# A first MLP whose last two token blocks share one in-projection through seven block products

## The chip, the cores and the metric

The kernel runs on one core of a Trainium2 chip. The metric is the device time of one execution in microseconds, as the median of several runs. A core has TensorE (PE: the matmul engine), VectorE (DVE), ScalarE (ACT), GpSimd (POOL) and SyncE (SP), which here issues the DMA transfers between DRAM and the on-chip memory in the order of its queue.

## What is computed

Retention attention gives 1536 tokens of 512 values; a first MLP with a gate (512 to 2048 to 512) and, behind an RMS norm, a second gated MLP (512 to 1536 to 512) follow.

```python
B, H, S, D = 2, 8, 768, 64
for t in range(S):                                  # attention
    state = gamma * state + outer(k[:, :, t], v[:, :, t])
    y[:, :, t] = scale * q[:, :, t] @ state
x = y as [1536, 512]
h = x @ w_in                                        # first MLP
x = (h * sigmoid(1.702 * h)) @ w_out
xn = x / sqrt(mean(x * x) + 1e-6) * rms_g           # second MLP
g = xn @ w_gate
out = (g * sigmoid(g) * (xn @ w_val)) @ w_out2
```

The weights arrive as 64-bit floats. Products are made in split form: each float32 operand is a high and a low part, and a product is three matmuls (high by high, high by low, low by high).

## The kernel before

**Tiles.** The tokens are three blocks of 512 (0, 1, 2), each of four chunks of 128 tokens for the attention. An MLP1 step (block j, f) takes one of 16 slices of 128 of the 2048 inner values: `mlp1_in` (line 400) makes h with the 12 matmuls of `in_proj` (L392), `mlp1_act` (406) the gate and its two halves on ACT and DVE (L408, L410, L411), and `mlp1_out` (415) adds the slice's part to the block's four sums with 12 matmuls (L369 to L371). All of these are 128x512.

**Weights.** SP loads half tiles of 64-bit words (`load_next`, L140), and `convert_next` (144) turns one of them into float32 with two ACT operations (L168, L169) and three DVE operations (L172, L173, L179). `halves` (373) splits a value: an ACT copy (L374) and a DVE subtraction (L375). In each step `split_in` and `split_out` (200, 204) split the in-weights of two steps on and the out-weights of the step, each 128x512; with 48 steps a slice is split once for every block. The 68 half tiles are converted beside MLP1 and the first part of MLP2, at a pace counted per step; those of MLP2 are written to DRAM and loaded again (`reload`, 187).

**Order.** `STEPS` (line 38) lists 48 steps: block 0 with f 0 to 7, block 1 with all, block 0 with f 8 to 15, block 2 with all. The attention of chunks 0 to 3 stands ahead; that of chunks 4 to 7 lies beside the first eight steps, that of 8 to 11 beside the second half of block 0, one task of `attention` (832) in a step, a chunk in two. A chunk has two POOL products (L230, L237) and a DVE operation for the low half of x (`x_low`, 319). The norms (`norm_tasks`, 446) and the operand sums of MLP2 (`x_tasks`, 502) lie beside block 2. A scheduler places each instruction in its engine's line from the order in which the code writes it and from the buffers of its pools: four 64-bit half tiles (`st`), two split out-weights (`wo`), four split in-weights (`wa`), fourteen temporary tiles (`tmp`).

**Seven products.** MLP2 already takes two blocks together through `seven` (655): a 2x2 arrangement of blocks of weights by blocks of tokens is made with seven products instead of eight, from sums of weight blocks (`set_tasks`, 571) and sums of token blocks (`x_tasks`). A product is 6 matmuls of 128x512 (L666) that add up in two banks; the results come out as sums with ACT copies (L673) and DVE additions. Two such chains run in turns, one in the banks of `ps_h`, one in those of `ps_t`; between them `fill` items do out-products.

## Time and profile before

| | us |
|---|---|
| median of 3 runs (602.67 to 603.08) | 602.86 |
| the profiled execution | 603.59 |
| its span on the core | 601.8 |
| PE busy | 594.8 |
| DVE busy | 445.5 |
| ACT busy | 356.2 |

The span is the time from the first to the last event of the core in the profiled execution; that execution's own time also has what lies around the span. Busy time is what an engine spends in instructions, an operation from its start to its end. Where instructions of an engine overlap, a single one's duration is longer than its share of the line; the distance from one start to the next (here: the pitch) is then the cost. The granted clock (PEclk) is TensorE's: 1.00 is 2.4 GHz.

### The profile page before, as it was taken

To read this page: it belongs to the slowest core of one execution; us is meant where nothing else is said; L and a number is where in the kernel's file an instruction comes from. 1 tells how busy PE (TensorE), PEld (TensorE's weight loads), DVE (VectorE), ACT (ScalarE), POOL (GpSimd) and SP (SyncE) were. 2 spreads that over 40 slices of the span, in tenths; PEclk is the share of its full clock that TensorE was granted. 3 is DMA by queue.
4 is the path that set the end of the run, shared out by engine and by line. 5 is a ranking of instruction groups with operands and counts; after the bars stand their busy time and mean duration, and the time that the engine had idled before them with its cause. 6 is when DMAs were issued, how large, how long until landed. Compare 5 with 4: busy or idle time off the path is not lost.

```text
span 601.8 us, 9259 instructions
## 1 busy us (share of the span) xinstructions
PE 594.8 (99%) x3354; PEld 495.2 (82%) x3354; DVE 445.5 (74%) x805; ACT 356.2 (59%) x685; POOL 29.6 (5%) x28
## 2 busy tenths in 40 slices
PE   8999999999999999999999999999999999999997
PEld 6777888888888878888887888898989889988885
DVE  2999968897797868989977999774655766655542
ACT  2577777786675666867757675453534535544532
POOL 4404100000112000000000000000000000000000
PEclk9999999999999999999999999999999999999999
DMA  8966724564577535436523513240211376643521
GB/s 328 354 207 245 247 87 139 162 203 133 179 228 244 175 118 149 114 106 205 180 106 105 174 54 116 78 139 20 95 63 71 108 256 230 211 143 106 173 71 70
DMA packets 32877, 93.14 MB, mean 155 GB/s; under 512 B 3904, under 2 KB 4160, under 8 KB 32832
## 3 DMA queue, kind: packets, MB, share of 16 engines
q1 hardware_dynamic: 32400, 92.42, 46.7%
q8 instruction: 26, 0.43, 0.3%
q10 hardware_dynamic: 432, 0.14, 0.1%
q14 instruction: 19, 0.16, 0.1%
HBM read 73.67 MB, written 18.87 MB: 154 GB/s over the span
## 4 chain that ended last, share of the span: by engine, by line
PE 94%; DVE 3%; DMA 1%; ACT 1%; issue 0%; SPq 0%; DVEq 0%
PE h L392 21%; PE acc L369 8%; PE acc L370 7%; PE acc L371 7%; PE o L369 5%; PE o L370 5%; PE o L371 5%; PE y L299 2%; PE sc L257 2%; PE y L286 1%; PE g2a L666 1%; PE g0a L666 1%; PE v0a L666 1%; PE v2a L666 1%; PE g10a L666 1%; PE g8a L666 1%
## 5 line engine op out<-in xcount | busy, mean ns | idle before, releaser
L369 PE MATMUL acc<-gh,woh 128*128 128x512 f32 x192 | 76.5, 399 | 0.0
L370 PE MATMUL acc<-gl,woh 128*128 128x512 f32 x192 | 74.9, 390 | 0.3 <-DVE gl L411 0.3
L371 PE MATMUL acc<-gh,wol 128*128 128x512 f32 x192 | 74.9, 390 | 0.0
L374 ACT ACTIVATE wih<-w 128x512 fp32r<-128x512 f32 x48 | 30.2, 631 | 56.5 <-PE h L392 53.2
L370 PE MATMUL o<-w3l,gh 128*128 128x512 f32 x144 | 56.2, 391 | 0.0
L369 PE MATMUL o<-w3h,gh 128*128 128x512 f32 x144 | 56.2, 391 | 0.0
L371 PE MATMUL o<-w3h,gl 128*128 128x512 f32 x144 | 56.1, 389 | 0.0
L375 DVE TENSOR_TENSOR wil<-w,wih 128x512 fp32r<-128x512 f32 x48 | 34.5, 719 | 20.6 <-ACT wih L374 20.4
L173 DVE CUSTOM_DVE_ANT_0 qw<-qw,uw 128x1024 uint16<-128x1024 uint16 x68 | 48.2, 712 | 0.6
L168 ACT ACTIVATE qw<-w 128x512 f32<-128x512 f32 x68 | 45.1, 663 | 0.6 <-DMA w<-in_w 0.6
L169 ACT ACTIVATE uw<-w 128x512 uint32<-128x512 uint32 x68 | 45.2, 665 | 0.0
L369 PEld LDWEIGHTS acc<-gh,woh 128*128 128x128 f32 x192 | 36.0, 188 | 8.6 <-issue 0.2
L370 PEld LDWEIGHTS acc<-gl,woh 128*128 128x128 f32 x192 | 36.1, 188 | 7.7 <-DVE gl L411 0.7
L374 ACT ACTIVATE woh<-w 128x512 fp32r<-128x512 f32 x48 | 30.1, 628 | 20.6 <-DVE w L179 13.8
L371 PEld LDWEIGHTS acc<-gh,wol 128*128 128x128 f32 x192 | 36.0, 188 | 7.6
L375 DVE TENSOR_TENSOR wol<-w,woh 128x512 fp32r<-128x512 f32 x48 | 32.8, 684 | 6.0 <-ACT woh L374 5.9
L375 DVE TENSOR_TENSOR gl<-gw,gh 128x512 fp32r<-128x512 f32 x24 | 16.6, 692 | 27.3 <-ACT gh L374 27.2
L172 DVE TENSOR_SCALAR qw<-qw 128x512 uint32<-128x512 uint32 x68 | 29.9, 441 | 8.8 <-ACT qw L168 8.8
L411 DVE SCALAR_TENSOR_TENSOR gl<-g,gh 128x512 fp32r<-128x512 f32 x48 | 34.1, 709 | 2.5 <-ACT gh L410 0.8
L374 ACT ACTIVATE gh<-gw 128x512 fp32r<-128x512 f32 x24 | 15.1, 631 | 29.0 <-PE o L370 24.9
L371 PEld LDWEIGHTS o<-w3h,gl 128*128 128x128 f32 x144 | 27.0, 188 | 5.6
L369 PEld LDWEIGHTS o<-w3h,gh 128*128 128x128 f32 x144 | 27.1, 188 | 4.8 <-ACT w3h L374 0.2
(1111 smaller groups left out, 1507.7 us busy)
## 6 DMA issues: line engine op xcount, KB each, us to landing
w<-in_w SPq DMA_DIRECT2D x68, 512.0 KB, 4.6
qk<-in_qk SPq DMA_DIRECT2D x12, 512.0 KB, 6.5
kv<-in_kv SPq DMA_DIRECT2D x12, 512.0 KB, 7.1
g0d<-gs SPq DMA_DIRECT2D x12, 256.0 KB, 2.0
g2d<-gl SPq DMA_DIRECT2D x12, 256.0 KB, 2.1
gw<-g0d SPq DMA_DIRECT2D x12, 256.0 KB, 2.7
gw<-g2d SPq DMA_DIRECT2D x12, 256.0 KB, 2.7
out<-o SPq DMA_DIRECT2D x11, 256.0 KB, 2.4
```

What stands on the lines that cost most here:

```text
L168: nc.scalar.activation(out=q, in_=high.bitcast(F32), func=ACTF.Copy, scale=2.0 ** -112)
L169: nc.scalar.activation(out=t, in_=low, func=ACTF.Copy, scale=2.0 ** -29)
L172: lambda: nc.vector.tensor_scalar(out=m, in0=m, scalar1=3, scalar2=None, op0=ALU.logical_shift_left),
L173: lambda: nc.vector.tensor_tensor(out=m, in0=m, in1=t, op=ALU.add),
L369: nc.tensor.matmul(out=out, lhsT=ah, rhs=bh, start=first, stop=False)
L370: nc.tensor.matmul(out=out, lhsT=ah, rhs=bl, start=False, stop=False)
L371: nc.tensor.matmul(out=out, lhsT=al, rhs=bh, start=False, stop=last)
L374: nc.scalar.activation(out=hi, in_=src, func=ACTF.Copy)
L375: nc.vector.tensor_tensor(out=lo, in0=src, in1=hi.bitcast(F32), op=ALU.subtract)
L392: nc.tensor.matmul(out=ps, lhsT=w[a][:, k * 128:(k + 1) * 128], rhs=x[b][:, k, :], start=o == order[0], stop=o == order[-1])
L411: nc.vector.scalar_tensor_tensor(out=lo, in0=g, scalar=1.0 / GELU, in1=hi.bitcast(F32), op0=ALU.mult, op1=ALU.subtract)
L666: nc.tensor.matmul(out=bank, lhsT=u, rhs=v, start=first and k == 0 and x == 0, stop=k == 1 and x == 2, skip_group_check=True,)
```

## The change

MLP1 is laid out anew. Block 0 runs through all 16 slices in a row (`for f in range(F1)`), with two conversions in a step and the attention of all eight remaining chunks beside it, one task in a step and a second one at f = 4 and f = 9. Its out-weights are split once, in a tile of 128x1024, and written to DRAM (512 KB a slice); the converted in-weights are written too (256 KB a slice). x of blocks 1 and 2 stays unsplit (`xr1`, `xr2`).

Then blocks 1 and 2 go through the in-projection as a pair: eight passes p of two slices, each a chain `seven` of seven products, in two lanes that stand three products apart (`LAG`). The token operands (four sums, seven splits of 128x1024, `m_tasks`) are made at the end of block 0 and through the first pass, the weight operands pass by pass (`set_tasks("wm", p)`). The gate of block 1 is split and its out-products run as `fill` items between the chains, with the split out-weights loaded again (`load_wo`, names `wowp`). The gate of block 2 is written to DRAM (`gm`, 256 KB a slice) and its out-products run in a last stretch of 16 steps of 12 matmuls, with gate (`gwm`) and weights (`wowq`) loaded again. The norm of block 0 lies beside the pair, that of block 1 and `x_tasks` beside the last stretch. Ten conversions more than before lie in MLP2. The diff, cut to its core:

```diff
...
-HALF = F1 // 2
-PARTS = [(0, 0, HALF), (1, 0, F1), (0, HALF, F1), (2, 0, F1)]
-STEPS = [(j, f, f == a, f == b - 1) for j, a, b in PARTS for f in range(a, b)]
-
-
-FIRST, OTHER, LAST = 1, 0, 2
+FIRST, OTHER, LAST = 0, 1, 2
+LAG = 3
...
-    wo_p = pool("wo", 2)
+    wo_p = pool("wo", 3)
...
-    tmp_p = pool("tmp", 14)
+    tmp_p = pool("tmp", 12)
...
+        elif half == 0:
+            p = i // 2
+            if i % 2 == 0:
+                kept["wm", p] = tc.dram_tile([128, 1024], F32, name=f"wm{p}d")
+            c = (i % 2) * 512
+            nc.sync.dma_start(out=kept["wm", p][:, c:c + 512], in_=dst.bitcast(F32))
...
+    def split_out(f):
+        t = wo_p.tile([128, 1024], F32R, tag="wo", name=f"wo{f}")
+        parts["wo", f] = both(t)
+        halves(*both(t), raw["w1", f][:, 512:1024].bitcast(F32))
+        kept["wo", f] = tc.dram_tile([128, 1024], F32, name=f"wo{f}d")
+        nc.sync.dma_start(out=kept["wo", f], in_=t.bitcast(F32))
+    def load_wo(f, user):
+        t = wo_p.tile([128, 1024], F32R, tag="wo", name=f"wo{user}{f}")
+        parts[user, f] = both(t)
+        nc.sync.dma_start(out=t.bitcast(F32), in_=kept["wo", f])
...
+            elif j == 1:
+                xt[j] = [x1_p.tile([128, KD, T], F32, tag="x11", name="xr1")]
+            else:
+                xt[j] = [xt_p.tile([128, KD, T], F32, tag="xt1h", name="xr2")]
...
-        x_low(c)
+        at.pop(("y", c))
...
+    def mlp1_item(key, j, f, m):
+        if j not in acc:
+            acc[j] = [psum(ps_a, f"acc{j}_{i}") for i in range(KD)]
+        w, g = parts[key, f], gt[key, f]
+        product(acc[j][m], [t[:, m * 128:(m + 1) * 128] for t in w], g, f == 0, f == F1 - 1)
...
+    def m_tasks():
+        xop["m"] = ops = {}
+        own = {1: "xt1l", 3: "xt0h", 4: "xt0l"}
+        def b(h, j):
+            return xt[1 + j][0][:, 2 * h:2 * h + 2, :]
+        def split(i, src):
+            if i in own:
+                t = xt_p.tile([128, KD, T], F32R, tag=own[i], name=f"xm{i}")
+                h, l = t[:, 0:2, :], t[:, 2:4, :]
+            else:
+                h, l = wide(f"xmh{i}", F32R), wide(f"xml{i}", F32R)
+            halves(h, l, src)
+            ops[i] = (h, l)
+        return sums_and_splits(b, split, lambda n: wide(f"m{n}"), lambda n: wide(f"m{n}"), b(0, 1))
...
+        if kind == "wm":
+            row = lambda i: raw["wm", g][:, 512 * i:512 * i + 512]
...
+    def use_m(p):
+        def use(i, j, src, own):
+            f = 2 * p + i
+            if j == 0:
+                nc.scalar.activation(out=own, in_=src, func=ACTF.Silu, scale=GELU)
+                gate_parts(("wp", f), own)
+                load_wo(f, "wp")
+                fill.extend((f, m) for m in range(KD))
+            else:
+                t = later["gs"].tile([128, T], F32, tag="gs", name=f"gm{f}")
+                nc.scalar.activation(out=t, in_=src, func=ACTF.Silu, scale=GELU)
+                to_dram("m", f, t)
+        return use
...
-    for i, (j, f, first, last) in enumerate(STEPS):
-        if i == 0:
-            att = [x for c in range(CPB, 2 * CPB) for x in attention(c)]
-        if i == HALF + F1:
-            att = [x for c in range(2 * CPB, 3 * CPB) for x in attention(c)]
+    att = [x for c in range(CPB, B * NC) for x in attention(c)]
+    sets = {}
+    def start_set(p):
+        reload("wm", p)
+        sets[p] = deque(set_tasks("wm", p))
+    def some(tasks, n):
+        for _ in range(min(n, len(tasks))):
+            tasks.popleft()()
+    for f in range(F1):
         begun = len(nc.cur_bb.bb.instructions)
-        k = min(i, len(STEPS) - 5)
-        if k <= HALF:
-            pace = min(2 * k + 4, k + HALF + 1, 2 * HALF)
-        elif k < F1:
-            pace = 2 * HALF + 13 * (k - HALF) // 8
-        else:
-            pace = k + HALF + 3 + (min(k, 32) - 8) // 3
-        while i and count["converted"] < pace:
+        while f and count["converted"] < min(2 * f + 4, 2 * F1):
             convert_next()
-        split_out(i)
-        if i:
-            split_in(i + 2)
-        ps = mlp1_in(i)
+        split_out(f)
+        if f:
+            split_in(f + 2)
+        if f == F1 - 3:
+            start_set(0)
+        if f == F1 - 2:
+            phase.close()
+            later["wb"] = side(ctx, "wb", 3)
+            later["gs"] = side(ctx, "gs", 3)
+            mops = deque(m_tasks())
+            start_set(1)
+            some(mops, 1)
+            some(sets[0], 1)
+        if f == F1 - 1:
+            some(mops, 4)
+            some(sets[0], 3)
...
+        if f in (4, 9):
+            next_of(att)
+    assert not att
+    lanes = [[(p, n) for p in range(k, F1 // 2, 2) for n in range(7)] for k in range(2)]
+    chains = {
+        p: seven(f"m{p}", ("wm", p), use_m(p), (ps_h, ps_t)[p % 2], xop["m"], T) for p in range(F1 // 2)
+    }
+    order = []
+    for t in range(len(lanes[0]) + LAG):
+        for k in range(2):
+            if 0 <= t - k * LAG < len(lanes[0]):
+                order.append(lanes[k][t - k * LAG])
...
+    mlp1_out("wo", 0, F1 - 1)
+    for m in range(KD):
+        evacuate(0, m)
+    norm = deque(norm_tasks(0, ps_h))
+    need = (1, 2, 5, 7, 8, 9, 11)
+    for e, (p, n) in enumerate(order):
+        if p == 0:
+            some(mops, need[n] - (11 - len(mops)))
+            if n < 3:
+                some(sets[0], 5)
+            some(sets[1], 2)
+        chains[p][n]()
+        while len(fill) > 4:
+            f, m = fill.popleft()
+            mlp1_item("wp", 1, f, m)
+        if p + 2 < F1 // 2:
+            if n == 0:
+                start_set(p + 2)
+            if n in (2, 3, 4, 5, 6):
+                some(sets[p + 2], 1)
+        if e > 12 and e % 2:
+            if count["converted"] < 2 * F1 + 20:
+                convert_next()
+        if e in (24, 32):
+            some(norm, 1)
+    some(norm, 1)
+    def wait_m(f):
+        if f < F1:
+            t = waiting["m", f] = later["gs"].tile([128, T], F32, tag="gs", name=f"gwm{f}")
+            nc.sync.dma_start(out=t, in_=kept_g["m", f])
+            load_wo(f, "wq")
+    def gate_m(f):
+        if f < F1:
+            gate_parts(("wq", f), waiting.pop(("m", f)))
+    while fill:
+        f, m = fill.popleft()
+        mlp1_item("wp", 1, f, m)
+        if f == F1 - 1:
+            evacuate(1, m)
+    some(norm, 1)
+    wait_m(0)
+    wait_m(1)
+    gate_m(0)
+    tasks = None
+    for f in range(F1):
+        wait_m(f + 2)
+        gate_m(f + 1)
+        some(norm, 2 if f == 0 else 1)
+        if f == 0:
+            norm += norm_tasks(1, ps_t) + x_tasks()
+        if f in (4, 6, 8, 10, 12):
+            some(norm, 1)
+        if f == 8:
+            for x in range(2):
+                reload("w2", x)
+        if f == 10:
+            sets = [set_tasks(k, 0) for k in ("wg", "wv")]
+        if f in (11, 13):
+            t = sets[(f - 11) // 2]
+            t[1]()
+            t[2]()
+        if f == F1 - 1:
+            some(norm, len(norm))
+            for n in (0, 3, 4):
+                for t in sets:
+                    t[n]()
+        mlp1_out("wq", 2, f)
...
-        for n in (1, 7, 13) if g >= JOIN else (1, 7):
+        for n in (1, 4, 7, 10) if g >= JOIN else (1, 4, 7):
...
```

How instructions stand on their engines, at three places. First PE in MLP1 after its first third: before, a step of block 2 (`h2_5` is its h of slice 5, `acc2_0` its first sum; `xt2h` and `xt2l` are the halves of x, `wih`/`wil` and `woh`/`wol` the split weights). Rows of before:

```order
L392 MATMUL h2_5_2868<-xt2l_1996,wih37_2728 128x512
L392 MATMUL h2_5_2868<-xt2h_1995,wil37_2729 128x512
L392 MATMUL h2_5_2868<-xt2h_1995,wih37_2728 128x512
L392 MATMUL h2_5_2868<-xt2l_1996,wih37_2728 128x512
L392 MATMUL h2_5_2868<-xt2h_1995,wil37_2729 128x512
L369 MATMUL acc2_0_2626<-gh36_2808,woh36_2785 128x512
L370 MATMUL acc2_0_2626<-gl36_2809,woh36_2785 128x512
L371 MATMUL acc2_0_2626<-gh36_2808,wol36_2786 128x512
```

Rows of after: the pair (`m3b` is the second bank of pass 3, `xmh2` and `xml2` the split token operand 2, `wm3xh` a split weight operand, `acc1_0` the first sum of block 1).

```order
L712 MATMUL m3b_2156<-xmh2_1687,wm3xh_1919 128x512
L712 MATMUL m3b_2156<-xml2_1688,wm3xh_1919 128x512
L712 MATMUL m3b_2156<-xmh2_1687,wm3xl_1920 128x512
L712 MATMUL m3b_2156<-xmh2_1687,wm3xh_1919 128x512
L712 MATMUL m3b_2156<-xml2_1688,wm3xh_1919 128x512
L712 MATMUL m3b_2156<-xmh2_1687,wm3xl_1920 128x512
L382 MATMUL acc1_0_1878<-gh3_2076,wowp3_2080 128x512
L383 MATMUL acc1_0_1878<-gl3_2077,wowp3_2080 128x512
L384 MATMUL acc1_0_1878<-gh3_2076,wowp3_2080 128x512
L382 MATMUL acc1_1_1879<-gh3_2076,wowp3_2080 128x512
```

A product of six matmuls on one operand stands where twelve on the four quarters of x stood, and block 1's out-products follow between two products of the chains.

Second, DVE where the second of the three block stretches begins. Before (`wol27`, `wil31`: low halves of out- and in-weights; `gl27`: of the gate; `qw`: conversion):

```order
L173 ISA qw311_2117<-qw311_2117,uw311_2118 128x1024
L375 TENSOR_TENSOR wol27_2128<-w111_1230,woh27_2127 128x512
L179 SCALAR_TENSOR_TENSOR qw311_2117<-w311_64_1886,qw311_2117 128x512
L375 TENSOR_TENSOR wil31_2297<-w115_1501,wih31_2296 128x512
L172 TENSOR_SCALAR qw240_2207<-qw240_2207 128x512
L411 SCALAR_TENSOR_TENSOR gl27_2192<-g27_2189,gh27_2191 128x512
L173 ISA qw240_2207<-qw240_2207,uw240_2208 128x1024
```

After (`gl15` is the last gate of block 0, `mt1`, `mt2`, `xr2`: token sums, `xml2`, `xml6`: low halves of token operands, `x1_0`: the finished sums of block 0, `swm0` and `wm0yl`: weight sums of pass 0 and their low half):

```order
L388 TENSOR_TENSOR xml2_1688<-xr1_516,xmh2_1687 128x1024
L579 TENSOR_TENSOR mt1_1691<-xr2_1131,xr1_516 128x1024
L421 SCALAR_TENSOR_TENSOR gl15_1724<-g15_1721,gh15_1723 128x512
L579 TENSOR_TENSOR mt2_1693<-xr2_1131,mt1_1691 128x1024
L579 TENSOR_TENSOR xr2_1131<-xr2_1131 128x1024
L446 COPY x1_0_1751<-acc0_1_545 128x512
L388 TENSOR_TENSOR xml6_1696<-mt2_1693,xmh6_1695 128x1024
L612 TENSOR_TENSOR swm0_1699<-wm0r_1560 128x256 x2
L612 TENSOR_TENSOR swm0_1699<-swm0_1699,wm0r_1560 128x256
L446 COPY x1_0_1751<-acc0_3_547 128x512
L612 TENSOR_TENSOR swm0_1699<-wm0r_1560,swm0_1699 128x256
L388 TENSOR_TENSOR wm0yl_1705<-swm0_1699,wm0yh_1704 128x512
```

The 1024-wide sums and splits of the pair's operands stand before and behind the last gate subtraction of block 0, where conversions and weight splits stood.

Third, the queue of SP where MLP1 ends. Before, in block 2 (`w33d`, `w28d`: converted weights written; `_64`: half tiles of words loaded):

```order
L185 DMA w33d_2781<-qw330_2774 128x512
L140 DMA w290_64_2783<-in_w2 128x512
L185 DMA w33d_2781<-qw331_2850 128x512
L140 DMA w291_64_2858<-in_w2 128x512
L185 DMA w28d_2910<-qw280_2903 128x512
L140 DMA w340_64_2912<-in_w3 128x512
L185 DMA w28d_2910<-qw281_2957 128x512
L140 DMA w341_64_2965<-in_w3 128x512
```

After, in the last stretch (`gwm`: gates of block 2, `wowq`: split out-weights, both loaded from what was written):

```order
L979 DMA gwm2_2983<-gmd2_2040 128x512
L979 DMA gwm3_3011<-gmd3_1990 128x512
L211 DMA wowq2_2985<-wo2d_584 128x1024
L979 DMA gwm4_3036<-gmd4_2191 128x512
L979 DMA gwm5_3062<-gmd5_2142 128x512
L211 DMA wowq3_3013<-wo3d_658 128x1024
L211 DMA wowq4_3038<-wo4d_743 128x1024
L979 DMA gwm6_3098<-gmd6_2358 128x512
L979 DMA gwm7_3130<-gmd7_2309 128x512
L211 DMA wowq5_3064<-wo5d_845 128x1024
```

Loads of 512 KB and 256 KB that the out-products of the next steps need stand where conversions were fed and written.

## Rows read from the trace of the kernel before

**Rows 1.** The page: busy time of each engine (share) xinstructions, and PE's busy tenths.

```profile
PE 594.8 (99%) x3354; PEld 495.2 (82%) x3354; DVE 445.5 (74%) x805; ACT 356.2 (59%) x685; POOL 29.6 (5%) x28
...
PE   8999999999999999999999999999999999999997
```

**Rows 2.** Windows: the stretch, its length, each engine's busy time, clock, DMA share, rate.

```profile
core 0: us, PE busy (x) PEld busy (x) DVE busy (x) ACT busy (x) POOL busy (x), PEclk, DMA share, GB/s
...
43.00:77.00 34.00, 34.00 (x254) 27.32 (x252) 32.92 (x55) 24.53 (x47) 8.48 (x5) 1.00 0.69 239
...
215.00:300.00 85.00, 85.00 (x423) 70.25 (x420) 77.26 (x143) 61.49 (x113) 0.00 (x0) 1.00 0.48 145
400.00:500.00 100.00, 100.00 (x546) 86.91 (x545) 60.70 (x123) 45.16 (x90) 0.00 (x0) 1.00 0.34 117
```

**Rows 3.** Chain of waits in MLP1: start, length, engine, output, line, how many instructions.

```profile
91.01 2.72 PE h L392 x12
96.45 2.72 PE h L392 x12
...
256.54 2.89 PE h L392 x12
```

**Rows 4.** Timeline of PE: first out-products of steps beside attention; start, length, operation.

```profile
40.25 0.50 PE L369 MATMUL acc<-gh,woh 128*128 128x512 f32 x1
...
54.72 0.50 PE L369 MATMUL acc<-gh,woh 128*128 128x512 f32 x1
```

**Rows 5.** Timeline of DVE beside block 2, without POOL: operations of four sizes.

```profile
287.81 1.21 DVE L375 TENSOR_TENSOR xl<-x,xh 128x1024 fp32r<-128x1024 f32 x1
288.94 0.68 DVE L375 TENSOR_TENSOR wil<-w,wih 128x512 fp32r<-128x512 f32 x1
289.54 0.41 DVE L172 TENSOR_SCALAR qw<-qw 128x512 uint32<-128x512 uint32 x1
289.88 1.21 DVE L551 TENSOR_TENSOR x<-x,t 128x1024 f32<-128x1024 f32 x1
...
298.17 0.41 DVE L580 TENSOR_TENSOR swg<-w20r,w21r 128x256 f32<-128x256 f32 x1
298.51 0.41 DVE L580 TENSOR_TENSOR swg<-swg,w20r 128x256 f32<-128x256 f32 x1
```

**Rows 6.** Groups of ACT: line, operation, count, busy, mean ns, idle before.

```profile
L410 ACT ACTIVATE gh<-g 128x512 fp32r<-128x512 f32 x48 | 30.0, 624 | 0.2
L408 ACT ACTIVATE g<-h 128x512 f32<-128x512 f32 x48 | 27.8, 579 | 0.0
```

**Rows 7.** Timeline of DVE and POOL beside the attention of block 1.

```profile
47.64 2.96 POOL L237 TENSOR_TENSOR kd<-kv,sm_sb 128x512 f32<-128x512 f32 x1 [19.32 <-DVE gl L411]
...
51.22 1.69 POOL L230 TENSOR_TENSOR qd<-qk,qd_sb 128x512 f32<-128x512 f32 x1 [0.63 <-DVE w L179]
51.67 1.79 DVE L411 SCALAR_TENSOR_TENSOR gl<-g,gh 128x512 fp32r<-128x512 f32 x1
53.54 1.42 POOL L237 TENSOR_TENSOR kd<-kv,sm_sb 128x512 f32<-128x512 f32 x1 [0.63 <-DVE gl L411]
53.98 1.60 DVE L172 TENSOR_SCALAR qw<-qw 128x512 uint32<-128x512 uint32 x2
```

**Rows 8.** DMA: issues (KB, median us to landing) of all and of 465:515; windows.

```profile
w<-in_w SPq DMA_DIRECT2D x68, 512.0 KB, 4.6
...
w35r<-w35d SPq DMA_DIRECT2D x2, 512.0 KB, 6.7
...
w211r<-w211d SPq DMA_DIRECT2D x1, 512.0 KB, 3.4
...
0.00:20.00 20.00, 18.40 (x218) 13.28 (x218) 8.75 (x15) 7.55 (x20) 8.98 (x15) 1.00 0.93 350
10.00:20.00 10.00, 9.92 (x166) 8.40 (x162) 7.46 (x13) 5.83 (x18) 6.50 (x6) 1.00 1.02 397
```

**Rows 9.** Groups by line: the score products of the attention.

```profile
L257 PE MATMUL sc<-qk 64*128 64x128 f32 x192 | 15.6, 298 | 1.0 <-DMA qk<-in_qk 0.7 <-DVE S_sb L354 0.2
```

More of the change, by code (lines that the diff above doesn't have):

```diff
@@ L123, in tile_retention_mlp_swiglu @@
     kept = {}
-    queue = []
-    for a, b in ((0, HALF), (HALF, F1)):
-        queue.append(("w1", a, 0))
-        for f in range(a, b - 1):
-            queue += [("w1", f + 1, 0), ("w1", f, 1)]
-        queue.append(("w1", b - 1, 1))
+    queue = [("w1", 0, 0)]
+    for f in range(F1 - 1):
+        queue += [("w1", f + 1, 0), ("w1", f, 1)]
+    queue.append(("w1", F1 - 1, 1))
     queue += [(kind, i, half) for kind, i in SECOND for half in range(2)]
@@ L413, in mlp1_act, with mlp1_out, evacuate @@
         )
[L415 to L420 removed]
+    def mlp1_act(f, ps):
+        g = tmp(f"g{f}")
+        nc.scalar.activation(out=g, in_=ps, func=ACTF.Silu, scale=GELU)
+        gate_parts(("wo", f), g)
+    def mlp1_item(key, j, f, m):
[3 more added lines that the diff above has]
+        product(acc[j][m], [t[:, m * 128:(m + 1) * 128] for t in w], g, f == 0, f == F1 - 1)
+    def mlp1_out(key, j, f):
         for m in range(KD):
[L422 to L424 removed]
+            mlp1_item(key, j, f, m)
     x1 = {}
[L428 removed]
+    def evacuate(j, m):
         if j not in x1:
             x1[j] = x1_p.tile([128, KD, T], F32, tag=f"x1{min(j, 1)}", name=f"x1_{j}")
[L432 to L439 removed]
+        if m % 2:
+            nc.vector.tensor_copy(out=x1[j][:, m, :], in_=acc[j][m])
+        else:
+            nc.scalar.activation(out=x1[j][:, m, :], in_=acc[j][m], func=ACTF.Copy)
     def wide(name, dtype=F32):
@@ L573, in set_tasks @@
         st = {}
-        c = 512 * (kind == "wv")
-        a = lambda i, h: raw["w2", g + i][:, c + 256 * h:c + 256 * h + 256]
+        if kind == "wm":
+            row = lambda i: raw["wm", g][:, 512 * i:512 * i + 512]
+        else:
+            c = 512 * (kind == "wv")
+            row = lambda i: raw["w2", g + i][:, c:c + 512]
+        a = lambda i, h: row(i)[:, 256 * h:256 * h + 256]
         def total(n, x, y, op):
@@ L590, in x @@
         def x():
-            halves(*part("x", wa_p, 512), raw["w2", g][:, c:c + 512])
+            halves(*part("x", wa_p, 512), row(0))
         def sums():
@@ L655, in seven @@
     def seven(name, key, use, p, ops, n):
-        w = wops[key]
+        w = wops.setdefault(key, {})
         st = {}
@@ L901, in tile_retention_mlp_swiglu @@
-    while norm:
-        next_of(norm)
-    for n in (0, 3, 4):
-        for t in sets:
-            t[n]()
+        if f:
+            mlp1_out("wo", 0, f - 1)
+        if f in (4, 9):
[10 more added lines that the diff above has]
+                order.append(lanes[k][t - k * LAG])
@@ L909, in tile_retention_mlp_swiglu @@
+    for m in range(KD):
+        evacuate(2, m)
     sorted_steps = [(n, k) for n in range(7) for k in range(2)]
@@ L940, in set_work @@
                 work[n + 2 * x + k].append(nxt[k][x])
-    mlp1_out(len(STEPS) - 1)
     reload("w3", 0)
```

88 lines of the change are left out of this document (21 added, 67 removed).

## The prediction

> **What bounds the kernel now.** I read the busy shares first. TensorE (PE) is busy 594.8 of 601.8 us [rows 1], with the granted clock at 1.00 in every stretch [rows 2], which is the 2.4 GHz level. So almost nothing is to be had from waits: 7.0 us in all, in the first and the last slices of the span [rows 1]. DVE, at 445.5 us, is the second engine [rows 1]; ACT has 356.2 and POOL 29.6.
>
> Then the stretches, since an average hides what is late. In all of these, from 43 us on, PE is busy for the whole of the stretch, whatever the others do; in 43–77, where attention and two conversions a step lie beside the first block's MLP1, DVE is busy for 32.92 of 34.00 us, in 215–300 for 77.26 of 85 [rows 2]. The reader is to see that PE stays full even where DVE is near its own limit. The chain of waits says the same: in the middle of MLP1 the in-projections follow each other every 5.44 us (91.01 to 96.45), each 2.72 us for 12 matmuls, and the out-products fill the rest [rows 3]. Hence one 128x512 matmul costs 2.72 / 12 = 0.2267 us of the span, though the groups show longer single ones, because they overlap. Time is saved by fewer matmuls, and lost by anything that makes the full PE line wait.
>
> **What is removed on PE.** Blocks 1 and 2 have 16 in-projections of 12 matmuls each, 384. As a pair they become 8 passes of 7 products of 6 matmuls, 336, of the same 128x512 shape. The out-products stay 192 per block, only later. All matmuls of the other shapes are as many as before. 48 x 0.2267 = 10.9 us, all on the path that sets the end. The sum is made from the profiled execution: 603.59 us, 601.8 of it span, 1.79 around it; it stands 0.73 above the median of the runs, 602.86. 603.59 - 10.9 = 592.7.
>
> **Block 0 (16 steps in a row, attention of eight chunks beside them): +1.0.** This is the load of 43–77 for twice as long. That load had DVE at 97% by durations; by pitches, start to start, a 512 operation takes 0.60, a 512 shift 0.34, a 256 sum 0.34, a 1024 one 1.13 [rows 5], and an overlap of some 0.08 between neighbours is gone. For two steps (one chunk of attention) I get four conversions of 0.34 + 0.60 + 0.60 = 1.54, six 512 operations for the splits and gates, two masks at 0.60 and a state update at 0.34, 6.16 + 3.6 + 1.2 + 0.34 = 11.3 us. PE needs 54.72 - 40.25 = 14.47 us for the same two steps [rows 4]. Beside a POOL operation DVE is stretched: a gate subtraction beside the 1.69 us POOL product took 1.79, two shifts beside the next, 1.42 long, took 1.60 [rows 7], where 0.68 and 0.34 + 0.41 [rows 5] are usual: 1.1 and 0.85, some 1.0 each, two per chunk, so 13.2 of 14.47 (a step with both tasks, f = 4 and 9, has 8.3 of PE's 9.04). The subtraction that made the low half of x is dropped for the eight chunks, which gives 0.6 per chunk back against before.
>
> Beside the first of these operations a rule of the Trainium skill can be weighed ("SBUF — State Buffer", section "SBUF: two separate sides"): GpSimd and a DVE operation that reads two SBUF inputs share a port pair as an exclusive lock, and the loser blocks until the other's instruction ends. The subtraction reads two SBUF tiles and was stretched by 1.1 of the POOL product's 1.69 us, which agrees in kind; by the whole lengths the two steps would come out as the slower rival below.
>
> New there are the DMA writes: per step 512 KB of split out-weights and 256 KB of raw in-weights, beside two loads of 512 KB and, on average, 400 KB of attention inputs. From the first of these writes to the last, the queue moves some 36.7 MB; the block is 16 steps of 24 matmuls (87 us) and eight chunks at 14.47 - 10.88 = 3.6 (29), together 116 us, so 316 GB/s. Stretches of before show 239 with no wait of PE and 350 over the first 20 us, at a share of 0.93 [rows 2, 8]; between 10 and 20 us it was 397 [rows 8]. It fits, at four fifths of the best. But loads will land later than the median 4.6 us [rows 8], nearer the 6.7 of a crowded stretch, and SP issues them behind writes that wait for DVE's splits. Bounds: 0 (nothing was lost in 43–77) to 2.5, two and a half times what the score products of all chunks waited in before, 1.0, of it 0.7 for DMA [rows 9]; I take 1.0, as much again.
>
> **The change from block 0 to the pair: +1.5.** Here the order puts 1024-wide operations into DVE's line: between the last gate subtraction of block 0 (gl15) and the split of the last total (xm4) stand 8 of 1024, 16 of 512, 15 of 256. By pitches 8 x 1.13 + 16 x 0.60 + 15 x 0.34 = 23.7 us; PE has 104 matmuls to run meanwhile, 23.6 us. So the two are level, and each product in between waits when its operand is late; gl15 itself stands behind a 1.13 us sum, and block 0's last out-products wait for it. The first out-product of block 1 waits for an addition (0.60), a silu (0.58) and a copy (0.62) [rows 5, 6] that nothing but the other lane covers: up to 1.4 once. By durations (1.21, 0.68, 0.41 [rows 5]) the DVE line is 27.1, 3.5 more than PE's. Bounds 0 and 4.3; I take 1.5, near the pitches, which are what a full DVE showed.
>
> **The pair's steady passes: nothing.** PE has 42 + 24 matmuls for a pass, 15.0 us. DVE has by pitches 2.5 conversions (3.9), four weight sums (1.4), their splits (2.1), three additions (1.8) and two gate subtractions (1.2), 10.4 us; ACT, less busy than DVE in every stretch [rows 2], has less. The out-weights come as one DMA of 512 KB, 3.4 us when alone [rows 8], issued some chains ahead of use. If that cover went, each of 16 loads could show 1 us; that is in the rivals.
>
> **The last stretch of block 2's out-products: +0.6.** Sixteen steps of 12 matmuls, 2.72 us each, each needing 512 KB of split weights and 256 KB of gate from DRAM: 768 KB in 2.72 us is 289 GB/s. There are three buffers for the weights, and a buffer is asked for again when its step ends. So the pitch is at least (landing + 2.72) / 3, which passes 2.72 when the landing passes 5.44 us. Alone a load lands in 3.4, in the crowded 465–515 stretch w35r took 6.7 [rows 8]. At 6.0 the pitch is 2.91, and 14 x 0.19 = 2.6 us are lost; at 6.7 it is 3.14, and 5.9 are. The queue holds little else in this stretch (no conversions), so I stay near the low end. The norms of blocks 0 and 1 also stand in PE's line there; before, those steps cost 2.89 instead of 2.72 [rows 3], 0.2 each, and I take 0.6 for all of it, bounds 0 to 5.9.
>
> **MLP2: nothing.** Its matmuls are untouched. It gets ten more conversions, 10 x 1.54 = 15.4 us of DVE; in 400–500 DVE is busy for 60.70 of 100 us and PE for 100.00 [rows 2], so the slack hides them four times over. If it did not, they would show as waits at gate products.
>
> **The sum.** 592.7 + 1.0 + 1.5 + 0.6 = 595.8 profiled; less the 0.73, **595.0 us** as the median.
>
> **Rivals.**
> 1. The covers hold everywhere: 592.7 - 0.7 = 592.0. For it: PE lost nothing at 97% DVE [rows 2]. Against it: three handovers that before does not have. Chance 0.13.
> 2. The stored weights come late. The last stretch runs at DMA's pace with landings near 6.7, so that up to 5.9 stand in place of the 0.6, and the handover costs up to 2.8 more: 595.0 - 0.6 + 4 to 8.7, 598.4 to 603.1. For it: 6.7 us landings in a crowd [rows 8]; against: little else is queued. Chance 0.15, a third of it within 0.2% of before.
> 3. Slower than before: DVE becomes the bound of block 0. If every POOL operation holds DVE for its whole length, two steps need 11.3 + 1.42 + 1.69 = 14.4, level with 14.47; with the longest seen, 2.96 and 1.69 [rows 7], 15.95. That is 1.48 beyond PE's 14.47, eight times: +11.9, so 592.7 + 11.9 + 2.1 - 0.7 = 606.0. Without it stand 594.1, 8.8 below before, so it turns the sign from 1.1 us per chunk beyond PE's time on. Against it: the same load ran in 43–77 with PE full [rows 2], and the x subtraction is gone. By the skill's lock rule as above this is what a full block would look like. Chance 0.09.
> 4. The change does not do what it says: chains wait on the bank handed from product to product, so that 7 products take as long as the 8 they replace: about 603, no change. MLP2 already runs such chains in two lanes with PE at 100.00 of 100 us in 400–500 [rows 2]. Chance 0.03.
>
> The forecast itself (593 to 598) has 0.60. A difference of 0.2%, 1.2 us, is about what a measurement of this kernel can tell from none: faster means under 601.65. Faster: 0.60 + 0.13 + the part of rival 2 that stays below, 0.10 = 0.83; same: 0.05 of rival 2 + 0.02 of rival 4 = 0.07; slower: 0.09 + 0.01 of rival 4 = 0.10. The range leaves out rivals 3 and 4 and the upper part of 2, 0.06, and little below: 591.5 to 601.0.
>
> **What would show it.** The profile after should have 3,306 PE instructions in place of 3,354, PE busy near 584, chains of 6 matmuls at 1.36 us in the pair stage, and PE idle in three places: short waits around gl15 and xml6 on DVE, a wait for the first wowp load or its gate, and waits of the wowq products for DMA if rival 2 holds. If PE waits in block 0 on DVE conversions or gates, by over 8 us in sum, rival 3 holds; if on loads whose landing is above 7 us, the DMA estimate was wrong. The forecast fails if block 0 takes over 119 us, the last sixteen steps over 46 us, or the pair's passes over 15.5 us each.

## The result, and the profile after

The changed kernel took 594.64 us (median of 4 runs, 594.38 to 595.33), the kernel before beside it 602.97: a ratio of 0.9863, interval 0.9846 to 0.988. That is 8.3 us less, where 7.9 were forecast (595.0). Run once more later on, as one of the experiments, it had a median of 596.51 with single runs from 593.67 to 598.51, a ratio of 0.9882 (0.986 to 0.9904): again below 1, and inside the forecast range, but with a spread of 4.8 us, where the eleven runs of the kernel before beside it lie within 2.1. Where that comes from is one of the things the experiments found.

The page of the changed kernel, part 1, answers to [rows 1]:

```profile
PE 584.7 (99%) x3306; PEld 486.2 (82%) x3306; DVE 450.5 (76%) x828; ACT 357.3 (60%) x684; POOL 26.1 (4%) x28
```

PE has 48 instructions and 10.1 busy us less; its idle time went from 7.0 to 7.9 us (span 592.6). The windows (columns as in [rows 2]) for block 0, the handover, the pair, the last stretch, and a stretch of MLP2:

```profile
33.00:137.00 104.00, 104.00 (x741) 83.60 (x740) 92.65 (x153) 75.47 (x142) 13.11 (x10) 1.00 0.93 327
137.00:165.00 28.00, 26.39 (x114) 20.86 (x114) 25.77 (x44) 18.40 (x31) 0.00 (x0) 1.00 0.48 170
165.00:259.00 94.00, 94.00 (x416) 77.68 (x415) 69.98 (x131) 66.01 (x122) 0.00 (x0) 1.00 0.87 290
259.00:314.00 55.00, 54.39 (x252) 44.31 (x251) 45.22 (x85) 30.23 (x54) 0.00 (x0) 1.00 0.83 288
391.00:491.00 100.00, 100.00 (x546) 86.97 (x545) 70.00 (x142) 51.32 (x102) 0.00 (x0) 1.00 0.41 142
```

The reader is to see two things. PE is full in block 0, in the pair and in MLP2, and lacks 1.61 us at the handover and 0.61 in the last stretch. And over the whole of block 0 DMA has a mean share of 0.93, at 327 GB/s; such a share had before only been seen in the opening [rows 8]. The list of PE's waits (us in all, times, longest) names what is missing:

```profile
PE acc L382 <- ACT gh L420: 1.2, 1, 1.2
...
PE acc L382 <- ACT x L448: 0.5, 1, 0.5
PE m0a L712 <- ACT wm0yh L387: 0.4, 1, 0.4
```

The chain of waits shows the pair as forecast, products of six matmuls in 1.36 us:

```profile
177.94 1.36 PE m2b L712 x6
179.30 1.36 PE m3a L712 x6
```

### The profile page after: what moved, and what is told of

Its sections match the earlier page's. It is cut to its first block, busy times and chain, and to the rows that moved or that the text cites. A ratio compares the mean times of both kernels' runs of the same rounds, so it can differ in the third digit from the quotient of the medians.

```text
span 592.6 us, 9365 instructions
## 1 busy us (share of the span) xinstructions
PE 584.7 (99%) x3306; PEld 486.2 (82%) x3306; DVE 450.5 (76%) x828; ACT 357.3 (60%) x684; POOL 26.1 (4%) x28
## 4 chain that ended last, share of the span: by engine, by line
PE 90%; DMA 5%; DVE 2%; ACT 2%; SPq 0%; issue 0%
PE acc L382 7%; PE h L405 7%; PE acc L384 7%; PE acc L383 6%; PE o L382 6%; PE o L383 6%; PE o L384 6%; DMA w<-in_w 2%; PE sc L265 1%; PE y L307 1%; PE y L294 1%; DMA qk<-in_qk 1%; DMA wowq<-wo11d 1%; PE g2a L712 1%; PE v2a L712 1%; PE g10a L712 1%
## 5 line engine op out<-in xcount | busy, mean ns | idle before, releaser
L383 PE MATMUL o<-w,gh 128*128 128x512 f32 x144 | 56.2, 390 | 0.0
L384 PE MATMUL o<-w,gl 128*128 128x512 f32 x144 | 56.1, 389 | 0.0
L382 PE MATMUL o<-w,gh 128*128 128x512 f32 x144 | 55.7, 390 | 0.0
L384 PEld LDWEIGHTS o<-w,gl 128*128 128x128 f32 x144 | 27.0, 188 | 5.6
L382 PEld LDWEIGHTS o<-w,gh 128*128 128x128 f32 x144 | 27.1, 188 | 4.7
L383 PEld LDWEIGHTS o<-w,gh 128*128 128x128 f32 x144 | 27.1, 188 | 4.6
L382 PE MATMUL acc<-gh,wo 128*128 128x512 f32 x64 | 26.0, 411 | 0.0
L382 PE MATMUL acc<-gh,wowq 128*128 128x512 f32 x64 | 25.2, 394 | 0.6 <-ACT x L448 0.5
L382 PE MATMUL acc<-gh,wowp 128*128 128x512 f32 x64 | 24.3, 393 | 1.2 <-ACT gh L420 1.2
L384 PE MATMUL acc<-gh,wowq 128*128 128x512 f32 x64 | 25.2, 394 | 0.0
L384 PE MATMUL acc<-gh,wo 128*128 128x512 f32 x64 | 25.1, 393 | 0.0
L383 PE MATMUL acc<-gl,wo 128*128 128x512 f32 x64 | 25.1, 393 | 0.0
L383 PE MATMUL acc<-gl,wowq 128*128 128x512 f32 x64 | 25.0, 391 | 0.0
L383 PE MATMUL acc<-gl,wowp 128*128 128x512 f32 x64 | 25.0, 390 | 0.0
L384 PE MATMUL acc<-gh,wowp 128*128 128x512 f32 x64 | 24.9, 389 | 0.0
```

The lines of the kernel that those rows point to most:

```text
L382: nc.tensor.matmul(out=out, lhsT=ah, rhs=bh, start=first, stop=False)
L383: nc.tensor.matmul(out=out, lhsT=ah, rhs=bl, start=False, stop=False)
L384: nc.tensor.matmul(out=out, lhsT=al, rhs=bh, start=False, stop=last)
```

## The experiments

All times are beside the kernel before on the same chip, 602.9 to 603.2. What a run has "more" is counted from 594.64, the changed kernel's first median; from its later one, 596.51, it would be 1.9 less. Small differences between medians near 595 say little, for the spread told above; there the waits in the profiles decide.

**Are the 48 matmuls the gain?** Product 7 of each pair pass is made twice:

```diff
             P(st["b"], 7, True)
+            if name[0] == "m":
+                P(st["b"], 7, True)
```

> The seventh product of each of the eight pair passes is made twice (the second starts the bank anew): 48 matmuls of 128x512 are back, all else is as in the changed kernel. If the matmuls of the full PE line set the time, as the prediction says: +48 x 0.2267 = +10.9, so 605.5 us (604.5 to 606.5), with PE busy near 595 and idle near 8 us. If the gain came mainly from what else the change takes away (32 splits of out-weights on ACT and DVE, the subtractions for x), the pair stage has slack on PE and the same matmuls cost under 5: below 600.

Measured: 606.86 (605.39 to 607.57), the profiled span 604.5, 11.9 above the 592.6 of the changed kernel; PE busy 595.3, 10.6 more. Between the two theories the one of the PE line holds; the median lies 0.4 above the range that it gave, the profiled run (606.3) inside it. With the matmuls back, the rest of the change is a loss: 606.86 is 3.7 above the kernel before beside it (603.15).

**How much room has DVE in block 0?** The low half of each out-weight is made four times:

```diff
         halves(*both(t), raw["w1", f][:, 512:1024].bitcast(F32))
+        hi, lo = both(t)
+        for _ in range(3):
+            nc.vector.tensor_tensor(out=lo, in0=raw["w1", f][:, 512:1024].bitcast(F32), in1=hi.bitcast(F32), op=ALU.subtract)
```

> In block 0 the subtraction of each out-weight split runs four times instead of once: 48 more DVE operations, 48 x 0.60 = 28.8 us by pitch. In the changed kernel DVE is busy for 92.65 of 104 us between 33 and 137; by pitches its 153 rows need some 12 less, about 80. If pitch is the right measure (the prediction's sum), there are 24 us to spare and the rest of 5 to 8 shows: 598 to 604, DVE full in block 0. If durations are, only 11 us were to spare: +17, about 612. If DVE is far from the path: 594.6.

Measured: 610.35 (608.42 to 611.35), 15.7 more. The window of block 0:

```profile
33.00:137.00 104.00, 100.75 (x701) 77.34 (x701) 103.73 (x176) 69.29 (x133) 19.53 (x10) 1.00 0.83 289
```

DVE is full and PE waits. Of 28.8 us added 15.7 were paid, so some 13 were to spare (15, counted from the later median): near the durations' 11, not the 24 of pitches alone. The prediction's own sum, which counted the POOL stretches (13.2 of 14.47 us per chunk, so 1.27 x 8 = 10), was the better one; my expectation here had left the stretches out.

**How much room has DMA in block 0?** Each split out-weight is written twice:

```diff
         nc.sync.dma_start(out=kept["wo", f], in_=t.bitcast(F32))
+        again = tc.dram_tile([128, 1024], F32, name=f"again{f}d")
+        nc.sync.dma_start(out=again, in_=t.bitcast(F32))
```

> Each split out-weight of block 0 is written to DRAM twice (512 KB more in each of 16 steps, 8.4 MB): between 33 and 137 the queues then have 34.0 + 8.0 = 42 MB in place of 34. If DMA still has room up to the 410 GB/s that landings of saturated moments show, 42 MB take 103 us and the cost is 0 to 2: up to 596.6. If the share of 0.93 at 327 GB/s means a limit near 352, block 0 takes 42 / 0.352 = 119 us: +15, about 610, with PE waiting on conversions whose loads land after 10 us and more.

Measured: 612.88 (610.57 to 614.0), 18 more. Windows, of block 0, of 20 us in it, and then of the handover:

```profile
33.00:137.00 104.00, 99.76 (x714) 78.96 (x714) 89.03 (x144) 71.69 (x135) 13.77 (x10) 1.00 0.97 356
...
43.00:63.00 20.00, 20.00 (x144) 15.67 (x143) 16.31 (x30) 14.38 (x29) 1.13 (x1) 1.00 1.03 407
...
145.00:150.00 5.00, 4.25 (x18) 2.62 (x16) 2.92 (x5) 2.02 (x4) 0.00 (x0) 1.00 1.03 418
150.00:155.00 5.00, 2.61 (x7) 1.66 (x6) 3.01 (x3) 1.54 (x2) 0.00 (x0) 0.74 0.86 320
155.00:160.00 5.00, 1.96 (x4) 0.52 (x3) 4.80 (x9) 2.44 (x4) 0.00 (x0) 0.50 0.65 257
160.00:165.00 5.00, 4.55 (x11) 3.34 (x12) 4.69 (x11) 4.70 (x9) 0.00 (x0) 0.50 0.00 0
```

The same 20 us in the changed kernel:

```profile
43.00:63.00 20.00, 20.00 (x154) 15.75 (x155) 17.42 (x30) 14.57 (x28) 4.03 (x3) 1.00 1.01 408
```

The mean rate over block 0 rose from 327 to 356, and neither theory holds as it was put. A limit near 352 it is not: from 43 to 63, where loads and writes are mixed, both kernels move 407 to 408 GB/s, and PE is full. Nor was there room for the added writes at a cost of 0 to 2. By the end of block 0's in-projections (142.06 against 136.08) 6 us were lost; PE's waits there are for masks and gates (3.4 us for DVE). The rest came at the handover. The pair's first weights landed after 8.8 to 10.6 us, the first token sum `mt` was made at 153.10 instead of 134.89, PE stood still, and the granted clock fell to 0.50, the 1.2 GHz level, for the matmuls that followed. How much of this is late landing and how much the order on the engines, no run here separates. On average block 0 takes four fifths of what DMA gives in its full stretches, 327 of 408 GB/s; the added writes show that this is not enough room for a quarter more.

**Is the third weight buffer needed?**

```diff
-    wo_p = pool("wo", 3)
+    wo_p = pool("wo", 2)
```

> The pool of split out-weights has two buffers instead of three, as in the kernel before. By the prediction's loop the last sixteen steps run at (landing + 2.72) / 2: with landings of 3.5 to 5.5, median near 4.5, a pitch of 3.6 and +14 us there; the pair's 512 KB loads may add 0 to 8: 608 to 617. If the third buffer isn't what covers the loads: 594.6 to 596.

Measured: 605.2 (603.27 to 607.57), 10.6 more, so it is, though less than expected. PE waits for loads several times, for `wowq` in the last stretch and for `wowp` in the pair:

```profile
PE acc L382 <- DMA wowq<-wo4d: 1.2, 1, 1.2
PE acc L382 <- DMA wowp<-wo13d: 1.1, 1, 1.1
PE acc L382 <- DMA wowq<-wo8d: 1.0, 1, 1.0
PE acc L382 <- DMA wowq<-wo6d: 0.9, 1, 0.9
```

The 16 loads of the last stretch are issued from 263.86 to 317.86, 3.6 us apart. That is the number expected, but not made up as expected: these loads landed in 3.2 to 4.7 us, with a median of 3.6, for which the loop gives (3.6 + 2.72) / 2 = 3.16. With three buffers the loads are 3.12 apart (261.71 to 305.34 for 14 steps), not 2.72, since norms and the first matmuls of MLP2 lie between and PE's wait ahead of the stretch falls in that time; the same 0.4 stands in both. The loss in that stretch is (3.6 - 3.12) x 15 = 7.2.

**What makes PE wait at the handover?** First only PE's order: the first out-products of block 1 are held behind two more products (`end` is the last PE instruction so far).

```diff
...
-        while len(fill) > 4:
+        while len(fill) > (8 if e < 8 else 4):
             f, m = fill.popleft()
+            begun = len(done)
             mlp1_item("wp", 1, f, m)
+            if f == 0 and m == 0:
+                for x in done[begun:]:
+                    after(x, end)
```

> The first out-products of block 1 (gate gh0, weights wowp0) are held behind two more products of the chains, so that PE doesn't stand before them for 1.21 us at 149. If the gate's chain of addition, silu and copy is the only late thing, the wait goes: -1.2, 593.4 against 594.6, and the profile has no wait of acc on gh. If DVE's line is what is late (in the changed kernel the low half xml7, which the next product needs, is made between 149.55 and 150.77), PE waits there instead for 1 to 1.6 us: 594.6, no change.

Measured: 596.98 (594.98 to 599.87). The wait for the gate is gone, and PE waits for xml7 instead, as DVE's theory said. Another wait, 0.5 in the changed kernel, has grown:

```profile
PE acc L382 <- ACT x L448: 3.0, 1, 3.0
PE m0b L712 <- DVE xml L388: 1.5, 1, 1.5
...
PE m0a L712 <- ACT wm0yh L387: 0.4, 1, 0.4
```

Then also the split of operand 7 earlier (three of the operand tasks at f = 14 instead of one):

```diff
-            some(mops, 1)
+            some(mops, 3)
             some(sets[0], 1)
```

> As the run with the held out-products, and the split of the token operand 7 (xml7) is asked for earlier, so that it stands right behind that of operand 6 in DVE's line, ahead of weight sums. If order in DVE's line is the matter: the 1.2 us go, 593.4. If the line is simply too full between 138 and 160 (its work of 23.7 us against PE's 23.6), the wait appears at another operand, most likely the weight sum's split wm0yh or xm3: 594.0 to 594.8.

Measured: 595.6 (594.21 to 596.91). The wait moved once more, to wm0yh, with 1.7 us. Then, from the changed kernel, block 0's copies on ACT:

```diff
-        if m % 2:
+        if m % 2 and j:
             nc.vector.tensor_copy(out=x1[j][:, m, :], in_=acc[j][m])
```

> The two copies of block 0's finished sums (0.60 each by pitch) go from DVE to ACT, nothing else changes by hand. If DVE's full line sets the waits at the handover (1.21 and 0.39): up to -1.2, 593.4. If the waits come from the order alone: 594.6.

Measured: 597.55 (595.49 to 599.81), with 0.9 on wm0yh and 0.9 on wm0yl. In the four orders (the changed kernel's and these three) the waits at the handover sum to 1.6, 1.9, 1.7 and 1.8 us. I took this for a full DVE line; the last experiment comes back to it.

**Does POOL hold DVE?** The product of k and its decay is made three times in six chunks:

```diff
+        for _ in range(2 if c >= CPB else 0):
+            nc.gpsimd.tensor_tensor(
+                out=t.rearrange("p (h d) -> p h d", h=H),
+                in0=ld["kv", c][:, 0],
+                in1=sm_sb[:, 0:H].to_broadcast([128, H, D]),
+                op=ALU.mult,
+            )
         at["kd", c] = t
```

> The POOL product of k with its decay is made three times instead of once in six chunks of block 0: 12 more POOL operations, some 18 us. By the stretches in the rows (1.0 us of DVE for a POOL operation of 1.5) DVE gets 12 us of load, and the run with repeated subtractions showed about 13 us of room (28.8 added, 15.7 paid): 594.6 to 597. If a POOL operation holds DVE for its whole length or longer: 18 us and more, +5 and up, 600 or above. If DVE runs on beside POOL: no stretch, 594.6, and DVE's busy time stays at 450.5.

Measured: 603.6 (602.29 to 607.06), 9 more: all of the gain. The timeline where four POOL operations follow each other:

```profile
87.70 1.36 POOL L238 TENSOR_TENSOR qd<-qk,qd_sb 128x512 f32<-128x512 f32 x1 [13.11 <-DMA qk<-in_qk]
87.84 1.77 DVE L428 SCALAR_TENSOR_TENSOR gl<-g,gh 128x512 fp32r<-128x512 f32 x1
89.02 1.50 POOL L245 TENSOR_TENSOR kd<-kv,sm_sb 128x512 f32<-128x512 f32 x1
89.53 1.53 DVE L167 CUSTOM_DVE_ANT_0 qw<-qw,uw 128x1024 uint16<-128x1024 uint16 x1
90.59 2.56 POOL L252 TENSOR_TENSOR kd<-kv,sm_sb 128x512 f32<-128x512 f32 x2
90.98 1.26 DVE L166 TENSOR_SCALAR qw<-qw 128x512 uint32<-128x512 uint32 x1
92.17 1.53 DVE L173 SCALAR_TENSOR_TENSOR w<-w,qw 128x512 uint32<-128x512 uint32 x1
```

DVE gets four operations done in the 5.9 us from 87.84, work of 2.1 by pitch. Over the whole run the price is lower: DVE's busy time rose by 8.7 us (450.5 to 459.2) where POOL's rose by 15.8 (26.1 to 41.9), 0.7 for each of the twelve. So the time came out as for the theory of whole lengths, but the load on DVE did not; it is even under the 12 us of the middle theory. That theory had the load about right, and wrong the time that it took to follow from it. My reading is that what is lost comes in one piece, so that the masks of the attention are late (PE y on DVE a, 4.8 us in sum in its list of waits) although DVE has room on average, 96.26 us busy of the 104 from 33 to 137. That is argued, not tested.

**What makes the spread?** The changed kernel once more:

> The changed kernel itself, beside the next two on the same chip. 594.6 us, as measured; if the wait before the last stretch (0.49 in its profile, 3.0 in the run with held out-products) depends on how late the gate load gwm1 lands, single runs spread upward by 2 to 4 us, up to 598.

Measured: 596.51 (593.67 to 598.51), and 1.7 us of wait for ACT's x. The mechanism is best read in the run with the 3.0 (held out-products), ACT's timeline where the last stretch begins:

```profile
266.97 0.63 ACT L420 ACTIVATE gh<-gwm 128x512 fp32r<-128x512 f32 x1 [3.26 <-DMA gwm<-gmd]
267.50 1.07 ACT L448 ACTIVATE x<-acc 128x512 f32<-128x512 f32 x2
```

ACT works in order. The split of gate 1 of block 2 stands ahead of the copies that free block 1's banks, and waits for a load; block 2's first sums wait for the banks. The chain of waits shows why the load is late: its buffer, one of three, still held a gate on its way to DRAM.

```profile
257.94 3.27 DMA gmd<-gm
...
261.29 5.66 DMA gwm<-gmd
```

In the changed kernel's first profile, with a wait of 0.49, the write took 3.72 us and the load 2.72; in the later one, with 1.7, the load took 4.14. So the write makes the wait, and how long the load itself takes sets how long the wait is. In the run with the 3.0 the granted clock was 0.67 from 269 to 274, after PE had been busy for 2.02 of the 5 us before, so that wait cost more than itself. The copies first:

```diff
...
         gate_m(f + 1)
+        if f == 0:
+            for x in nc.cur_bb.bb.instructions[begun:]:
+                if x.engine == mybir.EngineType.Activation:
+                    after(x, freed)
```

> On ACT the two copies that free block 1's banks stand ahead of the split of gate 1 of block 2, which waits for the load gwm1; before they stood behind it. If that order is what makes PE wait at 264 (0.49 us in one profile, 3.0 in another): no wait of acc on ACT's x, 594.0 to 594.4. A rival: the split of gate 1 then comes later and the second step of the last stretch waits for it instead, by as much: 594.6 or above.

Measured: 596.81 (594.31 to 599.17). The wait for the copies is gone; its place is taken by the next thing behind the splits in ACT's line, the norm's diagonal, a step that the rival did not name:

```profile
PE r L495 <- ACT diag L487: 2.0, 1, 2.0
```

So the order was the place of the wait and the late load its cause. The third run takes the load away: the last stretch begins with slices 15 and 14, whose gates stay on the chip (and the copies stand ahead of the split of gate 0).

```diff
+LAST_ORDER = [F1 - 1, F1 - 2] + list(range(F1 - 2))
...
-                to_dram("m", f, t)
+                if f < F1 - 2:
+                    to_dram("m", f, t)
+                else:
+                    waiting["m", f] = t
...
```

> The last stretch begins with slices 15 and 14, whose gates of block 2 are used from where they were made (no write, no load), then 0 to 13; the two copies stand ahead of the first split that waits for a load. If what is late at 264 is the way of a gate through DRAM (3.7 us for the write, 2.7 for the load, three buffers), both the wait for the copies and the one for the gates go: 593.5 to 594.2 with less spread between runs. If the three buffers then hold up the next gates: waits of acc on gates of slice 0 or 1, 594.6 or above.

Measured: 594.69 (593.6 to 594.95), and no wait in the last stretch. The four runs lie within 1.4 us, the changed kernel's six on the same chip within 4.8; but its first four lay within 1.0, and the two intervals of the ratio (0.9843 to 0.9869 here, 0.986 to 0.9904 there) overlap, so the profile says more here than the medians. The handover's 1.2 and 0.4 are still there.

**The handover again.** In the changed kernel DVE's timeline shows a gap ahead of the last gate of block 0, while the token sum behind it (`mt`, 138.82) had its inputs:

```profile
134.89 1.22 DVE L579 TENSOR_TENSOR mt<-xr,xr 128x1024 f32<-128x1024 f32 x1
138.21 0.69 DVE L421 SCALAR_TENSOR_TENSOR gl<-g,gh 128x512 fp32r<-128x512 f32 x1 [2.10 <-ACT gh L420]
138.82 1.22 DVE L579 TENSOR_TENSOR mt<-xr,mt 128x1024 f32<-128x1024 f32 x1
```

On top of the kept gates, that sum is put ahead of the gate on DVE, and the gate's copy ahead of a token copy on ACT (`t2`: the sum, `last`: the gate's operations):

```diff
...
+        if f == F1 - 1:
+            after(last[mybir.EngineType.DVE], t2)
...
             some(mops, need[n] - (11 - len(mops)))
+            for x in nc.cur_bb.bb.instructions[begun:]:
+                if x.engine in last:
+                    after(x, last[x.engine])
```

> On top of the run with the kept gates: DVE makes the token sum mt2 before the last gate subtraction of block 0 (gl15) instead of behind it, and ACT copies that gate's high half ahead of a 1.05 us token copy. In the changed kernel DVE stands idle for 2.10 us before gl15 at 136 to 138, while mt2 could run, and everything behind it is late by that. If this gap is what makes PE wait at the handover (1.21 and 0.39): both shrink to 0.6 or less in sum, 593.5 to 594.0 beside 594.7 of the run with the kept gates. If DVE's line is too full in any case: the waits come back at another operand with 1.5 us or more in sum, as they did in the two runs with other orders, 594.7.

Measured: 593.21 (592.54 to 593.72), a ratio of 0.9831 (0.9818 to 0.9845), the best of all. Its lead on the kept gates is at the edge of what the medians tell: the two intervals just touch. The profiled spans are only 0.4 us apart (591.4 and 591.8), since this profile has a wait of 0.7 for a load in the last stretch, the weights of slice 9. The gap is closed, and PE has no wait left at the handover. DVE's timeline:

```profile
135.37 1.22 DVE L581 TENSOR_TENSOR mt<-xr,xr 128x1024 f32<-128x1024 f32 x1
136.62 1.22 DVE L581 TENSOR_TENSOR mt<-xr,mt 128x1024 f32<-128x1024 f32 x1
137.79 0.69 DVE L422 SCALAR_TENSOR_TENSOR gl<-g,gh 128x512 fp32r<-128x512 f32 x1
...
144.44 0.69 DVE L389 TENSOR_TENSOR wm0yl<-swm,wm0yh 128x512 fp32r<-128x512 f32 x1 [1.26 <-ACT wm0yh L388]
```

The same stretch in the windows, beside 26.39 of 28.00 for the changed kernel:

```profile
137.00:165.00 28.00, 28.00 (x121) 21.91 (x120) 25.54 (x44) 19.43 (x33) 0.00 (x0) 1.00 0.50 179
```

That both waits went does not show that the gap had made them. What the longer one waited for, the gate's copy `gh` on ACT, came no earlier; what changed is PE's own line. First the changed kernel (DVE, ACT, PE), then this run (ACT, PE):

```profile
147.57 0.68 DVE L722 TENSOR_TENSOR pm<-m0b,pm 128x512 f32<-128x512 f32 x1
...
148.28 0.62 ACT L387 ACTIVATE wm1yh<-swm 128x512 fp32r<-128x512 f32 x1
...
149.33 0.62 ACT L387 ACTIVATE wm1zh<-swm 128x512 fp32r<-128x512 f32 x1
149.85 0.62 ACT L420 ACTIVATE gh<-pm 128x512 fp32r<-128x512 f32 x1
...
150.89 0.58 ACT L719 ACTIVATE pm<-m1a 128x512 f32<-128x512 f32 x1
...
150.52 0.96 PE L382 MATMUL acc<-gh,wowp 128*128 128x512 f32 x3 [1.21 <-ACT gh L420]
```

```profile
148.63 0.59 ACT L724 ACTIVATE pm<-m1a 128x512 f32<-128x512 f32 x1
...
150.15 0.63 ACT L421 ACTIVATE gh<-pm 128x512 fp32r<-128x512 f32 x1
...
149.27 0.50 PE L717 MATMUL m1a<-xmh,wm1yh 128*128 128x512 f32 x1
...
150.83 0.73 PE L383 MATMUL acc<-gh,wowp 128*128 128x512 f32 x2
```

Counted from the silu of block 0's last gate (at 136.11 and 136.49 on ACT), the copy starts 13.74 us later in the changed kernel and 13.66 here, and the low half xml7 (149.55 and 149.73) 13.44 and 13.24 later. DVE's gap has in part only moved: it stands still for 1.26 us before `wm0yl`. But the copy that frees the bank `m1a` now stands early in ACT's line (148.63 instead of 150.89), and so a product of six matmuls on that bank runs on PE from 149.27 to 150.83, just while the gate is made. The 1.21 us are covered by other work; they were not taken away. For the 0.39 on wm0yh the order of the sums may be the cause: that split starts 7.29 us after the silu, 7.83 before. What puts the copy of `m1a` earlier, the order on DVE or that on ACT, stays open, since both were changed at once.

## Why the prediction was right, step by step

The mechanism was right: fewer matmuls on a PE line that stays full. That the median came within 0.4 us of 595.0 is in part luck: single runs of the same kernel later lay between 593.67 and 598.51, the terms for lost time were too high at one place and right for other reasons at another, and the wait on ACT, which no term had, was 0.49 in the first profile and 1.7 in the later one.

- **Removed matmuls, 10.9.** Right: PE's busy time fell by 10.1, and putting 48 matmuls back cost 11.9 of span.
- **Block 0, +1.0.** Too high: PE is busy for 104.00 of 104.00 us. That DVE has about 10 us to spare was right (13 measured). "It fits, at four fifths of the best" was right too: 327 GB/s on average, 408 where DMA is full, and PE waits in neither. (The 36.7 MB are 2% above what the prediction's own figures for a step add up to, 35.9.) Nothing in the term says how near this is to too much: a quarter more cost 6 us in block 0 and 12 behind it.
- **The handover, +1.5.** The size was right, 1.21 + 0.39 in the profile, and the first out-product's wait of "up to 1.4" is the 1.21. The chain of addition, silu and copy was named; it took 2.9 us instead of 1.8 (147.57 to 150.47), with two splits of weight sums, wm1yh and wm1zh, between them in ACT's line. That DVE's line is level with PE's (23.7 and 23.6; the 27.1 by durations is 26.7 by its own figures) does not by itself make PE wait: in the last run PE has no wait over the same work. That the order on DVE made the wait is not shown; for the 0.39 it may be so.
- **The pair, 0.** Right: 94.00 of 94.00, and the first products of passes 3 to 7 follow each other every 15.0 us.
- **The last stretch, +0.6.** In the first profile 0.49, but for another reason. The weight loads landed in 3.1 to 6.2 us, mostly inside the 5.44 at which the loop breaks even, and the third buffer held them. The wait that the prediction lacks is the one of ACT for a reloaded gate ahead of the copies; it is 0.5 to 3.0 us long by run and can bring the clock down when it is long.
- **MLP2, 0.** Right: DVE's busy time in a stretch of 100 us rose from 60.70 [rows 2] to 70.00, and PE stayed at 100.00. (The slack of 39.3 us there is 2.6 times the 15.4 that were added, not four times.)
- **Its signs of failure.** Two of the three came up, although hardly any time was lost: block 0 took 119.2 us, from its first matmul at 22.17 to the pair's first at 141.35, where 119 was the bound, and the last sixteen steps 48.1 (265.22 to 313.31), where it was 46. PE waited for under 0.3 us in either. In the last sixteen steps other PE work lies between, 24 small matmuls of the norms and the first three of MLP2, which the bound did not count; what makes block 0 3 us longer than the 116 of the estimate was not looked into.
- **The rivals.** The slower one, DVE bound through POOL, did not come about, but is close: twelve more POOL operations gave the gain away. The Trainium skill ("SBUF — State Buffer", section "SBUF: two separate sides") gives a POOL operation, or a DVE operation with two SBUF inputs or in a two-port mode, the shared port pair exclusively for its whole instruction. Where POOL operations follow each other the trace agrees in kind, since DVE waits for most of each: 2.1 us of work took 5.9 beside 5.4 of POOL, also for a shift with one input tile (1.26 long in place of 0.41). No run here shows in which mode that shift ran.

## What to carry to other kernels

Where one engine is full, count its instructions first; that term decided the sign and nearly all of the size. Then look for the places where stages meet, because there in-order engines put work that is ready behind work that is not. Before the last stretch the wait of 0.5 to 3 us went when what is needed next was no longer sent through DRAM. At the handover 1.2 us went when PE had another product to run while the gate was made; its lateness stayed. Three changes of order there, and one before the last stretch, only moved a wait. So when a wait goes, read whether what it waited for came earlier, or whether something else now covers it, before you name the cause.
